# A delta-rule attention fused with a gated feed-forward layer: Gram products, first outputs and weight combinations put at other places of the order

## The chip, the cores and the metric

The kernel runs on one core of a Trainium2 chip. A core has a matrix engine (TensorE, PE in the profile; PEld is its loading of weights), a vector engine (VectorE, DVE), a scalar engine (ScalarE, ACT), a general one (GpSimd, POOL) and a sync engine (SyncE, SP), which here only issues transfers. Each engine runs its own list of instructions in order and waits on semaphores for the others. The metric is the time of one execution on the device in microseconds (us), lower is better.

## The reference

Attention with a state of 48x48 for each of 4 batches and 8 heads, over 768 steps, then a feed-forward layer with 384 inputs and 2048 hidden values:

```python
k_n = k / (np.linalg.norm(k, axis=-1, keepdims=True) + 1e-06)
for t in range(S):
    kt, vt, bt = (k_n[:, :, t], v[:, :, t], beta[:, :, t, None])
    y[:, :, t] = np.einsum('bhd,bhde->bhe', q[:, :, t], state)
    v_old = np.einsum('bhde,bhd->bhe', state, kt)
    state = state + bt[:, :, :, None] * np.einsum('bhd,bhe->bhde', kt, vt - v_old)
x = y.transpose(0, 2, 1, 3).reshape(B * S, H * D)
h = x @ w_in
g = h * (1.0 / (1.0 + np.exp(-1.702 * h)))
return g @ w_out
```

The weights w_in and w_out come as 64-bit floats. The kernel converts them to 32 bits on the device, on their bit patterns.

## The kernel before

**Units.** The 768 steps are cut in 6 chunks of 128. A unit is one chunk of one batch, for all 8 heads; units 0 to 3 are the four batches of the first chunk, units 4 to 7 those of the second, and so on to 23. Two units side by side (256 tokens) make one feed-forward block.

**One unit's work.** `turn` transposes k on PE, and `gram` makes G, the products of all keys of the chunk with each other (16 instructions on PE, then two copies out of PSUM: both on ACT for units 4 to 9, one on ACT and one on DVE for the others). `send_blocks` writes the four 32x32 diagonal blocks of G to DRAM with four transfers, and `load_diagonal` reads them back as `NT`, one block per partition. `invert` inverts them on DVE, for four or two units at a time, in many small steps; the inverses go through DRAM (`Yd`) and come back as `XB`. `Step` then solves for U in four block rows: `solve` multiplies a block row of V by its inverse (psU, copied by ACT to `US`), `below` multiplies by G (psR), and DVE subtracts that from the rows of V below. `queries` and `outputs` make the unit's output (psY) from the masked scores M (`select`, on POOL), and `state` adds to the state ST on DVE. The outputs go to `xT`, for two units together, partly by six small transfers (`xT<-last`).

**Order.** The file writes the order of the engines out by hand. Most operations go through wrappers that keep them in program order (so nearly every row of the profile names line 108); those that are called on `nc.gpsimd` or `nc.sync` directly may be moved by the scheduler, among them the adds of line 764. `together` interleaves the solving of one unit with the products of another; `hops(a, b)` is such a chain of eight for two units. The first four units have no feed-forward work beside them yet: units 0 and 1 are solved first, then 2 and 3. `warm(n)` puts n products whose result nobody reads on PE.

**Background work.** `fill(us)` takes the next pieces of a generator, `background`, until their estimated costs reach the number given: first the conversion of w_in (9 pieces), then the inversion for units 4 to 7 (`invert(1)`), then the conversion of w_out. One conversion (`conversion`) is a step on DVE, a scaling on ACT and four more steps on DVE; `conversions` weaves each piece with the next. Finished pieces set off the fetch of later ones (`fetches`): piece 1 the last quarter of w_in (12 transfers), piece 3 of w_in four row blocks of w_out (`fetch_out`), all on SP.

**Feed-forward.** `hidden` multiplies by w_in and applies the activation; its results go to tiles `gT` from a pool of six (`g_tile`), for the second block partly to `late_g`, which lies in the large scratch tile TW. The first two blocks are multiplied by w_out directly (`both_written`, `written`). From the third on, `seven` does it with seven products of quarter matrices in place of eight, which needs the combinations T1 = W12 - W11, T2 = W22 - T1, T3 = W22 - W12 (in place of W12) and T4 = W21 - T2 (`combined`: 16 adds on POOL). T1, T2 and T4 lie in TW, in its first, second and last third; `KX`, a spare place for a block of k, and the scores of some units lie in TW as well.

**Steady part.** `woven(n)` runs for n from 3 on: outputs of unit n-1, solving of n, scores of n+1, k of unit n+5 (`prepare`; from unit 12 on, k is scaled on POOL by `normalize`) and feed-forward work from `queue`, handed out by `spend`. `follow` issues the next loads and puts the next feed-forward block in the queue; the third block's `hidden` carries the combinations beside it (`beside_of`), one add for each of its steps.

Of the kernel before, what the change touches and what calls it, by code (L numbers as in the profile page):

```python
# [8 lines left out]
F32 = mybir.dt.float32  # L9
# [9 lines left out]
def kernel(  # L19
# [21 lines left out]
    B, H, S, D = q.shape  # L41
# [9 lines left out]
    NB = C // BS  # L51
    HB = 2
    NTH = HB * C
    FQ = 4
    GB = 6
    HF, HM = FC // 2, DM // 2

    XR = DP - D
    NW, NR, NA, NY, NU = 80, 11, 3, 28, 12
# [77 lines left out]
    def warm(n, after=None):  # L137
        ps = ps_moe.tile([128, 256], F32, tag="moe", name="ps_warm")
        if after is not None:
            after(ps[:, 0:1], 0.0)  # L140
        for _ in range(n):
            pe.matmul(ps, lhsT=ones[:, 0:128], rhs=ones, start=True, stop=True)
# [24 lines left out]
    def g_tile():  # L167

        return wk.tile([128, FQ, NTH], F32, tag="gT", name="gT", bufs=GB)
# [39 lines left out]
    def conversion(dst, raw, shape):  # L209

        lo, hi = raw[:, :, :, 0], raw[:, :, :, 1]
        ts, stt = vec.tensor_scalar, vec.scalar_tensor_tensor
        AND, OR = ALU.bitwise_and, ALU.bitwise_or
        E1 = 1 << 20
        p = dst.bitcast(I32)
        ts(p, hi, 0x7FF * E1, None, op0=AND)  # L220
        act.activation(p, p, ACT.Relu, scale=8.0, bias=low)
        yield 0.75
        stt(out=p, in0=hi, scalar=-(1 << 31), in1=p, op0=AND, op1=OR)
        yield 0.95
        ts(hi, hi, E1 - 1, E1, op0=AND, op1=OR)
        yield 0.7
        f = lo.bitcast(F32)
        stt(out=f, in0=lo.bitcast(U32), scalar=2.0**-32, in1=hi, op0=ALU.mult, op1=ALU.add)
        yield 0.95
        stt(out=dst, in0=f, scalar=2.0**-20, in1=dst, op0=ALU.mult, op1=ALU.mult)  # L230
        yield 0.95
# [27 lines left out]
    def conversions():  # L259

        whole = list(pieces())

        def begin(i):
            dst, raw, shape, name = whole[i]
            ops = conversion(dst, places[name[1]] if raw is None else raw, shape)
            return ops, next(ops)

        after, cost = begin(0)
        yield cost
        for i in range(len(whole)):  # L270
            ops = after
            yield next(ops)
            yield next(ops)
            if i + 1 < len(whole):
                after, cost = begin(i + 1)
                yield cost
            yield next(ops)
            cost = next(ops)
            done.add(whole[i][3])
            fetches.pop(whole[i][3], lambda: None)()  # L280
            yield cost
# [22 lines left out]
    def fill(us):  # L304
        while us > 0:
            us -= next(behind, us)
# [107 lines left out]
    def gram(n):  # L414

        c, b = units[n]
        kT = kTs[n]
        G = wk.tile([128, H, 128], F32, tag="G", name="G", bufs=6)
        pool_, tag = (ps_seq, "seq") if c == 0 else (ps_big, "big")
        ps = [pool_.tile([128, NP, 128], F32, tag=tag, name="psG") for _ in range(2)]  # L420
        for h in range(H):
            r = slice(h % 2 * 64, h % 2 * 64 + D)
            pe.matmul(
                ps[h % 2][:, h // 2], lhsT=kT[r, h // 2, :], rhs=kT[r, h // 2, :],
                start=True, stop=True,
            )
        act.activation(G[:, 0::2], ps[0], ACT.Copy)
        if B <= n < 2 * B + HB:
            act.activation(G[:, 1::2], ps[1], ACT.Copy)
        else:  # L430
            vec.tensor_copy(G[:, 1::2], ps[1])
        ready[n] = KN[n % len(KN)], kT, G
        return G

# [28 lines left out]
    def send_blocks(n, others=(), dma=sync):  # L463

        G = ready[n][2]
        Nd = dram.tile([H * C * BS], F32, tag="Nd", name="Nd", bufs=4)
        to = Nd.rearrange("(h p k) -> p h k", p=C, k=BS)
        for blk in range(NB):
            u = slice(blk * BS, (blk + 1) * BS)
            (beside if blk in others else dma)(out=to[u], in_=G[u, :, u])  # L470
        return Nd
# [291 lines left out]
    def add(o, a, b, op, engine=None):  # L763
# [2 lines left out]
    W11, W21 = w_out[:, 0:HF, 0:HM], w_out[:, HF:, 0:HM]  # L766
    W12, W22 = w_out[:, 0:HF, HM:], w_out[:, HF:, HM:]
    T1, T2, T4 = (
        TW[:, i * HF * HM : (i + 1) * HF * HM].rearrange("p (f d) -> p f d", f=HF) for i in range(3)
    )  # L770
    T3 = W12

    def combined():

        n = 2
        for o, a, b in ((T1, W12, W11), (T2, W22, T1), (T3, W22, W12), (T4, W21, T2)):
            for f in range(0, HF, n):
                add(o[:, f : f + n], a[:, f : f + n], b[:, f : f + n], sub_)
                yield

    def beside_of(work, other):

        for cost in work:
            next(other, None)
            yield cost
        run(other)

# [122 lines left out]
    def ahead_of(work, n):  # L910
        for _ in range(n):
            next(work, None)
# [34 lines left out]
    def follow(n):  # L947

        if n + 3 < len(units):
            load(n + 3, ((QP, q),))  # L950
        m = n - 1 + len(KN)
        if n == B + 1:
            nc.sync.dma_start(out=KN[m % len(KN)], in_=KX)
        elif n > B and m < len(units):
            load(m, ((KN, k),), nc.gpsimd.dma_start)
        if n - 1 + B < len(units):
            load_values(n - 1 + B)
        if n % HB == 0 and n > B:
            h = (n - 1) // HB
            gT, sums = [], []  # L960
            work = hidden(xTs[h], gT, slice(0, NTH), 1.3, sums)
            queue.append(beside_of(work, combined()) if h == HB else work)
            queue.append(seven(*units[h * HB], gT, sums))
            xTs.pop(h)

    debt = [0.0]

    def spend(cost):

        debt[0] = debt[0] + cost if queue else 0.0  # L970
        for done in take(debt[0]):
            debt[0] -= done
# [4 lines left out]
    def woven(n, share):  # L977

        nonlocal inverting
        A, B_, D_ = steps.pop(n - 1, None), steps.get(n), steps.get(n + 1) or NoStep()
        m = n + B + 1 if n > B else len(units)
        K = normalize(m) if m < len(units) and m >= 3 * B else iter(())
        P = prepare(m) if m < len(units) else iter(())
        if n == B:
            inverting = invert(*units[2 * B], HB)
        if n % HB == 1 and B + 1 < n and n + 1 + HB < len(units):
            inverting = invert(*units[n + 1 + HB], HB)  # L990
        ahead = FIRST[n] if n in FIRST else STEPS[:3] if n % HB == 1 else STEPS[3:]

        next(K, None)
        together([(B_, 1)], [(A, 2)])
        run(D_.scored)
        next(K, None)
        ahead_of(inverting, ahead[0])
        spend(share / 3)

        together([(A, 3), (D_, 0)], [(B_, 1)])  # L1000
        next(K, None)
        ahead_of(inverting, ahead[1])
        spend(share / 6)
        next(P, None)
        spend(share / 6)

        together([(B_, 2)], [(D_, 0)])
        if A:
            A.queries()
            A.outputs(True)  # L1010
        run(P)
        ahead_of(inverting, ahead[2])
        if n % HB == 0 and n > B:
            run(inverting)
        spend(share / 6)
        next(new_step(n + 2).scored, None)
        spend(share / 6)
        follow(n)
# [69 lines left out]
    pool.memset(late_U[:, H * D :], 0.0)  # L1088
    for s in pair:
        s.select()  # L1090

    def hops(a, b):

        yield [(a, 0)], []
        for blk in range(NB - 1):
            yield [(b, blk)], [(a, blk)]
            yield [(a, blk + 1)], [(b, blk)]
        yield [(b, NB - 1)], []

    def put_out(s):  # L1100
        s.queries()
        s.outputs(True, lambda: fill(1.7))
        steps.pop(s.n)

    path = hops(*pair[:2])
    for i in range(2 * NB):
        together(*next(path))
        if i in (1, 3):
            turn(B + HB + i // 2)
        if i < 2 * NB - 1:  # L1110
            warm(NU // 2 if i in (0, 1, 3) else NU)
        if i > 0:
            fill(1.7)
    for n in (B + 2, B + 3):
        gram(n)
        Ndx.append(send_blocks(n))
    load_diagonals(Ndx)
    for s in pair[:2]:
        put_out(s)
    sync(out=KN[0], in_=KX)  # L1120
    load(8, ((KN, k),), sync)
    for f in range(3):
        fetch_out(f)
    for n in range(B, B + 2):
        load(n, ((QP, q),), sync)
# [7 lines left out]

    gTs = [], []
    ffn.append(hidden(xTs[0], gTs[0], slice(0, NTH), 1.3))
    path = hops(*pair[2:])
    for i in range(2 * NB):
        together(*next(path))
        if i > 2:
            feed()  # L1140
        else:
            warm(NU // 2)
        fill(1.7)
    for s in pair[2:]:
        put_out(s)
# [79 lines left out]
```

## Time and profile before

| what | us |
|---|---|
| median of 3 runs | 781.2 (778.08 to 781.31) |
| the profiled execution | 772.88 |
| its span, first to last instruction | 771.2 |
| PE busy | 728.2 |
| DVE busy | 486.2 |
| ACT busy | 238.7 |
| POOL busy | 237.8 |

The engines in 40 slices of 19.3 us each (a digit is the busy share in tenths, 9 is 90% or more; PEclk is the clock that TensorE was granted):

```profile
PE   9288899989997999999999999999999999999998
PEld 7266778845676888898888988988998988988987
DVE  4896699999677577687677677777766850110000
ACT  3363444533332422322322323323322323212120
POOL 5022001300066442542542632632710601403123
PEclk9579899999998999999999999999999999999999
```

The program opens with units 0 to 3 and the weights' conversion (to about 186 us); from there on the woven part runs to the end. The median of the runs is 8.3 us above the profiled execution; durations below come from the profiled one.

### The profile page before, as it was taken

How to read it: one execution, taken by the hardware profiler on the slowest of the kernel's cores; microseconds unless marked ns; L12 is line 12 of the kernel's file. 1: busy time of each engine (PE TensorE's matmuls, PEld its weight loads, DVE VectorE, ACT ScalarE, POOL GpSimd, SP SyncE). 2: the span in 40 equal slices, each digit the busy share in tenths (PEclk: the TensorE clock that was granted, in tenths of full speed). 3: DMA queues.
4: the chain of work that ended last, by engine and by line, in shares of the span. 5: the costliest groups of instructions: out<-in, count | busy, mean ns of one | idle time of the engine just before them, and what ended most of it. 6: DMA issues, size and time to landing. Idle time of an engine off the chain costs nothing.

```text
span 771.2 us, 19686 instructions
## 1 busy us (share of the span) xinstructions
PE 728.2 (94%) x8451; PEld 624.0 (81%) x8451; DVE 486.2 (63%) x1014; ACT 238.7 (31%) x527; POOL 237.8 (31%) x210
## 2 busy tenths in 40 slices
PE   9288899989997999999999999999999999999998
PEld 7266778845676888898888988988998988988987
DVE  4896699999677577687677677777766850110000
ACT  3363444533332422322322323323322323212120
POOL 5022001300066442542542632632710601403123
PEclk9579899999998999999999999999999999999999
DMA  9985555541222113113113113123122120000000
GB/s 169 150 150 122 157 132 77 133 124 42 51 49 60 35 26 84 37 28 83 36 30 80 36 35 77 36 43 68 37 44 57 22 54 2 2 27 1 26 1 20
DMA packets 128182, 47.11 MB, mean 61 GB/s; under 512 B 117920, under 2 KB 122144, under 8 KB 128096
## 3 DMA queue, kind: packets, MB, share of 16 engines
q1 hardware_dynamic: 125568, 41.54, 26.1%
q0 software_dynamic: 1344, 3.93, 2.3%
q8 instruction: 66, 1.08, 0.6%
q10 hardware_dynamic: 1184, 0.39, 0.2%
q14 instruction: 20, 0.16, 0.1%
HBM read 33.13 MB, written 11.01 MB: 57 GB/s over the span
## 4 chain that ended last, share of the span: by engine, by line
PE 74%; DVE 13%; DMA 4%; issue 3%; SPq 2%; POOL 2%; ACT 1%; ACTq 0%; DVEq 0%; POOLq 0%
PE ph L108 27%; PE po L108 25%; PE psY L108 5%; PE psU L108 4%; PE psQ L108 4%; PE psG L108 3%; DVE w_out L108 3%; PE psT L108 2%; DVE P L108 2%; SPq L108 2%; DVE YB L108 2%; PE ps_warm L108 2%; PE psR L108 2%; DVE w_in L108 1%; DVE V L108 1%
## 5 line engine op out<-in xcount | busy, mean ns | idle before, releaser
L108 PE MATMUL ph<-xT,w_in 128*128 128x256 f32 x1152 | 264.0, 385 | 0.2 <-DMA xT<-last 0.2
L108 PEld LDWEIGHTS ph<-xT,w_in 128*128 128x128 f32 x1152 | 216.0, 191 | 32.4 <-DVE V L108 1.4
L108 PE MATMUL po<-w_out,gT 128*128 128x192 f32 (+1 forms) x736 | 147.2, 354 | 4.1 <-DVE o L108 3.6
L764 POOL TENSOR_TENSOR gT<-gT 128x512 f32<-128x512 f32 x80 | 106.5, 1340 | 124.1 <-ACT gT L108 113.6
L108 DVE TENSOR_TENSOR V<-V,psR 64x384 f32<-64x384 f32 (+1 forms) x96 | 53.3, 556 | 133.9 <-PE psR L108 132.6
L108 PEld LDWEIGHTS po<-w_out,gT 128*128 128x128 f32 x736 | 121.2, 191 | 19.6 <-DVE o L108 4.6
L108 ACT ACTIVATE gT<-ph 128x512 f32<-128x512 f32 x92 | 54.9, 596 | 143.4 <-PE ph L108 143.2
L108 DVE TENSOR_TENSOR P<-NT,YB 64x2 f32<-64x2 f32 (+9 forms) x200 | 95.3, 476 | 6.2
L108 DVE TENSOR_REDUCE YB<-P 64x2 f32<-64x2 f32 (+9 forms) x200 | 81.8, 409 | 6.9
L108 PE MATMUL po<-TW,gT 128*128 128x192 f32 x480 | 83.0, 328 | 0.0
L108 ACT COPY US<-psU 32x384 f32<-32x384 f32 x92 | 43.3, 470 | 127.1 <-PE psR L108 115.9
L108 PEld LDWEIGHTS psU<-V,XB 32*32 32x32 f32 x1536 | 57.0, 105 | 30.6 <-issue 12.7
L108 PEld LDWEIGHTS po<-TW,gT 128*128 128x128 f32 x480 | 77.9, 190 | 1.1 <-issue 0.3
L108 PE MATMUL psU<-V,XB 32*32 32x48 f32 x1536 | 67.8, 202 | 5.7 <-DVE V L108 3.5
L108 PE MATMUL psR<-US,G 32*32 32x48 f32 x2208 | 60.0, 203 | 3.2 <-ACT US L108 3.2
L108 DVE TENSOR_TENSOR o<-o,po 128x192 f32<-128x192 f32 x40 | 13.5, 351 | 75.8 <-PE po L108 75.3
L108 PEld LDWEIGHTS psR<-US,G 32*32 32x32 f32 x2208 | 50.7, 105 | 4.3 <-ACT US L108 3.9
L633 POOL TENSOR_SCALAR_AFFINE_SELECT M<-M 128x1024 f32<-128x1024 f32 x19 | 22.3, 1175 | 92.9 <-DVE M L108 61.0
L108 DVE TENSOR_TENSOR P<-NT 64x512 f32<-64x512 f32 (+7 forms) x50 | 44.5, 890 | 2.0
L93 POOL DMA_DIRECT2D KN<-in_k_dram x12 | 11.5, 958 | 84.1 <-PE psY L108 84.1
L108 PE MATMUL psQ<-QS,kT 48*128 48x176 f32 (+1 forms) x368 | 33.7, 324 | 1.6 <-ACT QS L108 1.6
L108 PE MATMUL psG<-kT 48*128 48x128 f32 x384 | 32.3, 304 | 2.5 <-ACT G L108 2.1
(118 smaller groups left out, 747.1 us busy)
## 6 DMA issues: line engine op xcount, KB each, us to landing
V<-in_v_dram SPq DMA_DIRECT2D x24, 192.0 KB, 3.1
out_dram<-o SPq DMA_DIRECT2D x24, 192.0 KB, 2.4
QP<-in_q_dram SPq DMA_DIRECT2D x22, 192.0 KB, 3.4
raw<-in_moe_w_out_dram SPq DMA_DIRECT2D x9, 384.0 KB, 3.9
NT<-Nd SPq DMA_DIRECT2D x24, 128.0 KB, 2.8
XB<-Yd SPq DMA_DIRECT2D x24, 128.0 KB, 3.1
Nd<-G SPq DMA_DIRECT2D x92, 32.0 KB, 1.7
Yd<-NT SPq DMA_DIRECT2D x22, 128.0 KB, 2.2
```

Of the source, the lines that this page charges most:

```text
L93: dma(out=place(dst, n)[:, :, 0:D], in_=src[b, :, c * C : (c + 1) * C, :].rearrange("h p d -> p h d"),)
L108: return lambda *a, **kw: tc.keep_in_program_order(op(*a, **kw))
L633: (pool if self.n < B else nc.gpsimd).affine_select(out=self.M, in_=self.M, compare_op=ALU.is_gt, fill=0.0, base=0, pattern=[[0, H], [1, 1 ...
L764: (engine or nc.gpsimd).tensor_tensor(o, a, b, op=op)
```

## The change

Seven edits. The scaling on ACT inside a conversion is issued at the beginning of the next fill rather than at the end of the step before it. G of units 0 and 1 lies in two tiles of the gT pool, so that units 6 and 7 find free buffers for theirs. The fetch of w_out's first row block and a fill of 3.3 us stand ahead of the hops. The Gram products of units 6 and 7, with their transfers of blocks, stand inside the hops of units 0 and 1 (after the fifth and sixth), where warming products go. The outputs of unit 0 come ahead of unit 1's last solve, and those of unit 1 after the first solve of unit 2. The hops of units 2 and 3 lose that first one and get longer warming. And T1 and T4 exchange their thirds of TW; the first four adds (T1) are issued in `woven(6)`, and the third block's `hidden` begins with four steps without adds.

```diff
 def conversion(dst, raw, shape):
     ts(p, hi, 0x7FF * E1, None, op0=AND)
+    yield 0.75
     act.activation(p, p, ACT.Relu, scale=8.0, bias=low)
-    yield 0.75
+    yield 0.0
...
 def conversions():
     after, cost = begin(0)
+    next(after)
...
             after, cost = begin(i + 1)
             yield cost
+            next(after)
...
 def gram(n):
-    G = wk.tile([128, H, 128], F32, tag="G", name="G", bufs=6)
+    G = (
+        g_tile().rearrange("p f (o t) -> p (f o) t", o=2) if n < HB
+        else wk.tile([128, H, 128], F32, tag="G", name="G", bufs=6)
+    )
...
 T1, T2, T4 = (
-    TW[:, i * HF * HM : (i + 1) * HF * HM].rearrange("p (f d) -> p f d", f=HF) for i in range(3)
+    TW[:, i * HF * HM : (i + 1) * HF * HM].rearrange("p (f d) -> p f d", f=HF) for i in (2, 1, 0)
 )
...
 def beside_of(work, other):
-    for cost in work:
-        next(other, None)
+    for i, cost in enumerate(work):
+        if i >= FQ:
+            next(other, None)
         yield cost
...
-        queue.append(beside_of(work, combined()) if h == HB else work)
+        queue.append(beside_of(work, combining) if h == HB else work)
...
+combining = combined()
...
 def woven(n, share):
     next(P, None)
+    if n == B + HB:
+        ahead_of(combining, HF // 2)
     spend(share / 6)
...
 for s in pair:
     s.select()
+fetch_out(0)
+fill(3.3)
...
-path = hops(*pair[:2])
+path, later = hops(*pair[:2]), hops(*pair[2:])
 for i in range(2 * NB):
     together(*next(path))
     if i in (1, 3):
         turn(B + HB + i // 2)
-    if i < 2 * NB - 1:
-        warm(NU // 2 if i in (0, 1, 3) else NU)
-    if i > 0:
+    if i in (4, 5):
+        gram(B + HB + i - 4)
+        Ndx.append(send_blocks(B + HB + i - 4))
+    elif i < 2 * NB - 2:
+        warm(NU if i == 2 else NU // 2)
+    if 0 < i < 2 * NB - 1:
         fill(1.7)
-for n in (B + 2, B + 3):
-    gram(n)
-    Ndx.append(send_blocks(n))
+    if i == 2 * NB - 2:
+        put_out(pair[0])
 load_diagonals(Ndx)
-for s in pair[:2]:
-    put_out(s)
+together(*next(later))
+warm(NU // 2)
+put_out(pair[1])
 sync(out=KN[0], in_=KX)
 load(8, ((KN, k),), sync)
-for f in range(3):
+for f in range(1, 3):
     fetch_out(f)
...
-path = hops(*pair[2:])
-for i in range(2 * NB):
-    together(*next(path))
+for i in range(1, 2 * NB):
+    together(*next(later))
     if i > 2:
         feed()
     else:
-        warm(NU // 2)
+        warm(NU)
     fill(1.7)
```

## The prediction

> **What bounds the kernel now.** I read the profile in this order: busy shares and the 40 slices, then busy time by stage, then the chain of waits, then the timelines of single engines around the places where TensorE (PE) is not busy. By stage (columns: stretch in us, length, then busy us and count for PE, PEld, DVE, ACT, POOL, then granted clock, DMA share, GB/s):
>
> ```profile
> 66.00:85.00 19.00, 14.89 (x353) 12.05 (x341) 18.16 (x28) 8.63 (x15) 0.00 (x0) 0.98 0.49 119
> 85.00:94.00 9.00, 9.00 (x158) 8.40 (x162) 3.52 (x8) 3.93 (x11) 0.00 (x0) 0.67 0.77 206
> 94.00:109.00 15.00, 13.54 (x304) 9.98 (x291) 14.17 (x22) 7.79 (x12) 0.00 (x0) 1.00 0.60 150
> 109.00:157.00 48.00, 46.72 (x300) 39.29 (x298) 45.36 (x101) 20.69 (x43) 8.14 (x5) 1.00 0.49 95
> 157.00:186.00 29.00, 25.05 (x223) 15.27 (x225) 26.89 (x66) 8.27 (x17) 1.09 (x1) 0.94 0.33 87
> 242.00:246.00 4.00, 0.03 (x1) 0.00 (x0) 3.63 (x12) 0.60 (x1) 1.31 (x2) 0.82 0.00 0
> 246.00:254.00 8.00, 7.95 (x90) 6.50 (x93) 3.71 (x8) 1.19 (x2) 0.00 (x0) 0.67 0.01 2
> 300.00:771.00 471.00, 464.30 (x5347) 416.07 (x5345) 252.13 (x532) 126.81 (x283) 158.99 (x122) 1.00 0.16 36
> ```
>
> From 300 us on PE is busy 464 of 471 us at clock 1.00: nothing there is touched, and time won earlier is kept. From 66 to 109 DVE paces (the solving hops with weight conversions between them), except 85 to 94, where DVE does 3.5 us of work in 9. From 109 to 157 both PE and DVE are full. At 242 PE stands for 4 us and then runs 8 us at a mean clock of 0.67. These two holes, with DVE's idle time before 66, are what the change can win. DVE's holes, and the work that ends the first stage:
>
> ```profile
> 66.38 1.14 DVE L108 TENSOR_TENSOR V<-V,psR 32x384 f32<-32x384 f32 x2 [7.06 <-PE psR L108]
> ...
> 90.17 0.36 DVE L108 TENSOR_TENSOR ST<-psY,ST 128x192 f32<-128x192 f32 x1 [4.84 <-PE psY L108]
> ...
> 109.14 1.22 DVE L108 TENSOR_TENSOR NT<-NT,bI 128x1024 f32<-128x1024 f32 x1
> ```
>
> **Hops of units 0 to 3 (first part).** The fill of 3.3 us after the masks puts four conversion steps (about 0.6, 0.6, 0.95, 0.9 us start to start, from the same steps at 67.5 to 71.8) into the 7.06 us before 66.38. Their cover is that idle time; their data was fetched before 53 us. The hops keep their pace, one DVE subtraction (1.14 or 0.56 us) and two or three conversion steps, so that I step along DVE's new order with those durations: subtractions at 66.4, 69.7, 72.7, 75.3, 77.7 and 79.7 us (80.45 before). The Gram products of units 6 and 7 (16 products, 1.16 us on PE, two copies of 0.6 on ACT) now stand behind hops 4 and 5. On ACT they stand ahead of the next hop's copy of U, which hop 6 waits for; by the durations that moves hop 6 to 78.8 on PE, while DVE is busy until 79.7: hidden, and 1 us on the path if that cover were gone. 24 warming products (of 84) go; they were fillers. The outputs of unit 0 then run under two fills (2.8 us of steps), its state addition comes at 83.1 instead of 90.17, and unit 1's waits for ACT's copies (0.54 + 0.47 + 0.47) and 1.7 us of PE, which puts it at 86 instead of 91.97. There, DVE idles about 1.6 us in place of 5.9.
>
> What is late next is the transfer of `xT`, for which the first hidden products stand in PE's order ahead of the remaining hops. On SP it stands behind the four loads of w_out and the diagonals:
>
> ```profile
> 82.03 2.35 SPq L108 DMA_DIRECT2D w_out<-in_moe_w_out_dram  x4
> 85.30 5.38 SPq L108 DMA_DIRECT2D Nd<-G  x8
> 90.77 1.79 SPq L108 DMA_DIRECT2D NT<-Nd  x4
> 92.76 4.79 SPq L108 DMA_DIRECT2D xT<-last  x6
> ```
>
> Now it is: eight blocks of units 4, 5, one raw row block, twelve w_in loads (6.7 us, to 75.5), four blocks of unit 6 (its Gram copies end at 77.6, so to 79.5), four w_out loads (to 81.9 in place of 84.4), four blocks, four diagonals, `xT`. The chain of waits shows the last w_out load landing at 90.36, 6.0 us after its issue, so 87.9 now. The fourth diagonal waits for that; `xT` follows at 88.4 and lands 7.06 us later as before (92.76 to the products at 99.82), at 95.4. So hidden products start 4.4 us sooner, and DVE's last subtractions, which then wait for hop 4 behind them, put the first step of the second inversion at 104.2 instead of 109.14. Since PE and DVE are both full after it, I count the lesser: **minus 4.4 us**. Bounds: minus 7 (DVE's order alone, without `xT`, gives 102.1), and 0, if w_out's loads land no sooner than before.
>
> G of units 0, 1 in two buffers of gT costs nothing: the next users of these buffers, hidden products from 95 on, come 10 us after the last reader. Scaling on ACT issued one fill later stands behind the copies of U; its readers on DVE come a hop later (2.0 us at the least, 0.94 for the scaling): 0.
>
> **Combinations of w_out (second part).** Each add takes about 1.0 us on POOL. In the built order two of the first combination's four (those clear of KX) move ahead of unit 5's mask, to where their w_out rows are converted, about 162 us less the gain. There DVE paces and POOL disturbs it: beside one POOL mask of 1.09 us at 179.41 a product of 64x8 took 0.77 us where its neighbours took 0.15 to 0.18. I take 0.6 us for each: **plus 1.2 us**; bounds 0 and 2. The Trainium skill (SBUF — State Buffer, § Who interferes with whom) has the pair of ports shared by these engines locked for a whole instruction; that would be 1 us for each, and the sum 0.8 us later. The trace agrees with the blocking, and shows less than a whole instruction lost.
>
> The mask itself waits for nothing new, and is needed 40 us later (the output products at 221.85). The other two adds and the third combination run between 212 and 222, when POOL did nothing or the same adds, and PE paces. The gain is here:
>
> ```profile
> 227.35 0.97 POOL L93 DMA_DIRECT2D KN<-in_k_dram  x1
> ...
> 231.12 0.83 POOL L320 TENSOR_TENSOR ksq<-KN 128x384 f32<-128x384 f32 x1 [1.76 <-DMA Nd<-G]
> ...
> 240.64 1.67 POOL L325 TENSOR_TENSOR rn<-ssq,half 128x8 f32<-128x8 f32 x1
> 244.99 1.01 POOL L329 TENSOR_TENSOR KN<-KN,rn 128x384 f32<-128x384 f32 x1 [2.68 <-DVE rn L108]
> ```
> ```profile
> 238.92 0.73 DVE L108 TENSOR_TENSOR P<-NT,YB 64x18 f32<-64x18 f32 x1
> ...
> 241.45 0.23 DVE L108 TENSOR_TENSOR P<-NT,YB 64x72 f32<-64x72 f32 x1
> ```
>
> PE waits at 242.03 for unit 12's k, scaled by POOL at 244.99; POOL waits there for DVE's `rn`, which stands behind nine inversion steps. In the new order the load of k is issued after two adds that can run from 223 (unit 5's mask is read by then), at 225 instead of 227.35; it lands 3.8 us later, and four adds follow instead of seven: 228.8 + 0.8 + 4.0 + 1.1 + 1.7 = 236.4 for POOL's power, in place of 242.3. Then POOL is still when DVE's steps run (from 235.3, set by a diagonal that stands where it stood). Four products that took 0.84, 0.74, 0.73 and 0.82 us take 0.16 to 0.19, and the scaling ahead of them 1.22 for 1.55: 2.7 us sooner. PE's wait shrinks from 4.02 to 1.3 us: **minus 2.7 us** (bounds 0 and minus 4). After the wait the clock was 0.50 from 245 to 251, and 18 hidden products took 6.2 us where 3.9 is usual (260.39): with the transposes 2.6 us lost. Waits of 0.67 us (at 289) left the clock at 1.00, one of 3.3 us (165 to 168) did not. At 1.3 us I take the former: **minus 2.6 us**; bounds 0 and minus 2.6.
>
> **Sum.** -4.4 + 1.2 - 2.7 - 2.6 = -8.5 us. The profiled execution took 772.88 us (span 771.2 and 1.7 around it), so 764.4; the median of the runs shown is 781.2, 8.3 above it, and I put the same sum on it: 772.7 us.
>
> **Rivals.** (a) The hole at 242 stays, since the diagonal that DVE waits for until 235.3 doesn't move, and DVE might still be disturbed: only -3.2, 778. Against it: POOL's chain is 6 us shorter. (b) The hops' gain is lost because the transfers ahead of `xT` share the bandwidth (206 GB/s from 85 to 94) and land as late as before: 781.2 + 1.2 - 5.3 = 777. For it: twelve w_in loads now lie just ahead. (c) All bounds at their best: -12.4, 769. (d) The change does not take the adds off the late place: excluded by the built order. (e) Slower: SP's one queue. Diagonals and `xT` wait for w_out's last load. If the twelve w_in loads (1.5 MB) and these four (1.6 MB) shared their way so that they moved at the 119 GB/s of 66 to 85, they would take 26 us from 69, to 95, and `xT` would land at 102.6, 2.8 us late: with the other terms no net effect. At the 87 GB/s of 157 to 186 they end at 104.6 and `xT` lands at 112.1, 12.3 us late: 12.3 + 1.2 - 5.3 = plus 8.2, 789. It decides against the change once the last load lands after 96.4. Against it: the same loads ran at 176 to 352 GB/s when queued together.
>
> **Chances.** Forecast 0.58; (b) 0.12; (a) 0.10; (c) 0.07; (e) 0.08; 0.05 for no net effect. About 0.5% (3.9 us) is what a measurement of this kernel can tell from no change. Faster: forecast, (c) and (b), nearly all: 0.76. Within: (a) and no net effect, 0.16. Slower: 0.08. The range 765 to 780 takes in (a), (b), (c) and leaves out (e) and the tail.
>
> **What would show it.** In the changed profile: conversions on DVE between 59 and 63 us; unit 0's state addition near 83; first hidden products near 95; the second inversion's first step near 104; POOL's power for unit 12 some 6 us ahead of DVE's `rn`; PE's wait before that transpose below 2 us and the clock 1.00 after it. I am wrong if `xT` lands after 99 us, if DVE's conversions between 157 and 186 lengthen by more than 2 us, or if PE still stands 3 us or more at that transpose.

## The result, and the profile after

The changed kernel took 769.8 us (median of 4 executions, 768.4 to 771.2), the kernel before beside it 781.2 us (4 executions, 778.1 to 782.6): a ratio of 0.987, 95% interval 0.983 to 0.991, 11.5 us by the medians. The forecast was 772.7 us, 8.5 us less. Two later repetitions, with many more executions of the kernel before beside them, gave 0.990 each (0.986 to 0.995, and 0.987 to 0.993): some 7.6 us.

The profiled execution of the kernel before (772.9 us) lay 8 us under the median of its own runs, and that of the changed kernel (771.2 us) was the longest of its four, so the two executions set side by side show 1.6 us and not the difference of the medians. That is why the readings below go by differences inside a trace, and by several traces.

Busy time by stage, changed kernel (length, then busy us and count of PE, PEld, DVE, ACT and POOL, granted clock, DMA share, GB/s):

```profile
66.00:85.00 19.00, 16.24 (x366) 13.56 (x367) 14.73 (x23) 8.91 (x16) 1.04 (x1) 0.75 0.79 148
85.00:94.00 9.00, 9.00 (x163) 8.01 (x160) 4.06 (x8) 2.99 (x9) 0.00 (x0) 0.58 0.75 234
94.00:109.00 15.00, 13.39 (x269) 10.10 (x268) 12.86 (x20) 6.11 (x12) 0.00 (x0) 0.89 0.54 126
109.00:157.00 48.00, 48.00 (x316) 40.58 (x316) 45.09 (x100) 21.78 (x45) 8.90 (x5) 1.00 0.49 93
157.00:186.00 29.00, 25.32 (x201) 15.89 (x201) 27.91 (x62) 8.47 (x18) 4.16 (x3) 0.88 0.33 90
242.00:246.00 4.00, 3.20 (x49) 2.47 (x37) 3.53 (x13) 1.55 (x4) 0.00 (x0) 1.00 0.25 49
246.00:254.00 8.00, 6.89 (x122) 5.91 (x124) 5.81 (x12) 1.66 (x3) 1.00 (x1) 1.00 0.01 2
```

The second hole is as forecast: from 246 to 254 the clock is 1.00, not 0.67, and PE stands 1.9 us, not 4.0. In the hops the forecast is not met: the clock is 0.75 from 66 to 85 (0.98 before) and 0.89 from 94 to 109 (1.00 before). DVE's timeline there:

```profile
60.74 0.68 DVE L108 TENSOR_SCALAR w_out<-w_out 128x768 int32<-128x768 int32 x1
61.34 1.49 DVE L108 TENSOR_SCALAR w_in<-w_out 128x768 int32<-128x768 int32 x1
62.76 1.57 DVE L108 SCALAR_TENSOR_TENSOR w_out<-w_out 128x768 f32<-128x768 uint32 x1
64.36 1.72 DVE L108 SCALAR_TENSOR_TENSOR w_in<-w_out,w_in 128x768 f32<-128x768 f32 x1
68.76 1.14 DVE L108 TENSOR_TENSOR V<-V,psR 32x384 f32<-32x384 f32 x2 [2.67 <-PE psR L108]
...
87.15 0.36 DVE L108 TENSOR_TENSOR ST<-psY,ST 128x192 f32<-128x192 f32 x1
93.25 0.36 DVE L108 TENSOR_TENSOR ST<-psY,ST 128x192 f32<-128x192 f32 x1 [4.42 <-PE psY L108]
...
111.73 1.22 DVE L108 TENSOR_TENSOR NT<-NT,bI 128x1024 f32<-128x1024 f32 x1
```

Four conversion steps now fill the idle time ahead of the first subtraction (2.67 us of idling left of 7.06). That subtraction comes 2.4 us later than in the trace of the kernel before (68.76 against 66.38); PE's first products wait for the transfer of the inverses (XB) there, in both kernels. Unit 0's state addition no longer waits, but unit 1's waits 4.42 us for PE's output products, which run at half clock, and the second inversion's first step comes at 111.73 us, where 104.2 was forecast and 109.14 was before (42.97 us behind the first subtraction, 42.76 before). `xT` is late with it. SP's queue:

```profile
83.86 1.78 SPq L108 DMA_DIRECT2D w_out<-in_moe_w_out_dram  x4
85.73 2.70 SPq L108 DMA_DIRECT2D Nd<-G  x4
88.53 4.73 SPq L108 DMA_DIRECT2D NT<-Nd  x4
94.04 4.58 SPq L108 DMA_DIRECT2D xT<-last  x6
```

POOL's list around unit 12, and PE behind it, first in the changed kernel and then in the kernel before:

```profile
228.53 0.97 POOL L93 DMA_DIRECT2D KN<-in_k_dram  x1
...
239.25 2.65 POOL L328 TENSOR_TENSOR rn<-ssq,half 128x8 f32<-128x8 f32 x1
246.05 1.00 POOL L332 TENSOR_TENSOR KN<-KN,rn 128x384 f32<-128x384 f32 x1 [4.15 <-DVE rn L108]
```
```profile
247.11 0.66 PE L108 MATMUL psT<-ident,KN 128*128 128x128 f32 x4 [1.91 <-POOL KN L332]
247.60 4.05 PE L108 MATMUL ph<-xT,w_in 128*128 128x256 f32 x18
```
```profile
246.05 1.12 PE L108 MATMUL psT<-ident,KN 128*128 128x128 f32 x4 [4.02 <-POOL KN L329]
246.96 6.22 PE L108 MATMUL ph<-xT,w_in 128*128 128x256 f32 x18
```

POOL is done with its power at 241.9 and idles 4.15 us until DVE's `rn`: it is DVE that is awaited now. The 18 hidden products take 4.05 us, 6.22 before.

### The profile page after: what moved, and what is told of

It is laid out like the page before. It is cut to its first block, busy times and chain, and to the rows that moved or that the text cites. A ratio compares the mean times of both kernels' runs of the same rounds, so it can differ in the third digit from the quotient of the medians.

```text
span 769.5 us, 19639 instructions
## 1 busy us (share of the span) xinstructions
PE 729.1 (95%) x8427; PEld 625.3 (81%) x8427; DVE 489.3 (64%) x1014; ACT 238.7 (31%) x527; POOL 242.3 (31%) x210
## 4 chain that ended last, share of the span: by engine, by line
PE 73%; DVE 16%; issue 3%; POOL 3%; DMA 3%; SPq 1%; ACT 0%; DVEq 0%; POOLq 0%; ACTq 0%
PE ph L108 27%; PE po L108 24%; PE psY L108 6%; PE psU L108 5%; DVE P L108 4%; DVE w_out L108 3%; PE psQ L108 3%; DVE YB L108 3%; PE psG L108 2%; PE ps_warm L108 2%; PE psR L108 2%; DVE NT L108 2%; PE psT L108 2%; DVE raw L108 1%; SPq L108 1%
## 5 line engine op out<-in xcount | busy, mean ns | idle before, releaser
L108 PEld LDWEIGHTS psU<-V,XB 32*32 32x32 f32 x1536 | 59.8, 108 | 30.0 <-issue 15.9
L108 PE MATMUL psU<-V,XB 32*32 32x48 f32 x1536 | 70.4, 207 | 5.5 <-DVE V L108 3.0
L108 PE MATMUL psR<-US,G 32*32 32x48 f32 x2016 | 55.8, 205 | 3.6 <-ACT US L108 3.6
L108 PEld LDWEIGHTS psR<-US,G 32*32 32x32 f32 x2016 | 47.2, 106 | 4.6 <-ACT US L108 4.3
L93 POOL DMA_DIRECT2D KN<-in_k_dram x12 | 11.5, 958 | 81.6 <-PE psY L108 81.6
L108 DVE TENSOR_REDUCE NT<-P 64x32 f32<-64x512 f32 (+9 forms) x50 | 33.4, 668 | 1.7
```

Source lines behind the costliest of these rows:

```text
L93: dma(out=place(dst, n)[:, :, 0:D], in_=src[b, :, c * C : (c + 1) * C, :].rearrange("h p d -> p h d"),)
L108: return lambda *a, **kw: tc.keep_in_program_order(op(*a, **kw))
```

## The experiments

Each run gave a trace. To read them together I cut each into four pieces: **a** from the first subtraction of the hops to the second inversion's first step, **b** from there to unit 5's output products (those of its masked scores, `psY<-TW,US`), **c** from there to unit 12's transposes, **d** from there to the end of the span (us); ahead of them the mean granted clock from 64 to 112 us. The time ahead of the first subtraction is in no piece: it was 66.2 to 70.5 us, and PE's first products wait there for XB to land, in the kernel before too (1.39 and 0.82 us in its second trace, where it was 68.1).

```
kernel                       clock    a      b      c      d     ratio to before (95%)
before, first trace          0.93  42.76 112.71  24.20 525.15
before, second (b_again)     0.83  46.47 112.86  24.13 525.14   0.999 (0.995 to 1.003)
before + warming (b_warm)    1.00  42.33 112.62  23.64 525.31   0.999 (0.996 to 1.002)
before + warming at unit 12  0.89  43.12 113.74  24.11 522.52   0.994 (0.991 to 0.997)
combinations only            0.93  42.70 113.07  21.77 522.47   0.993 (0.988 to 0.997)
hops' part only              0.96  40.69 112.60  24.03 524.88   0.994 (0.991 to 0.998)
changed, first trace         0.79  42.97 113.64  21.74 522.39   0.987 (0.983 to 0.991)
changed, second (a_again)    0.93  38.77 113.69  21.74 522.50   0.990 (0.986 to 0.995)
changed, third (a_third)     0.86  39.66 114.77  21.79 522.48   0.990 (0.987 to 0.993)
changed, xT first (a_xt)     0.82  41.22 114.83  21.99 522.45   0.991 (0.988 to 0.994)
changed, no fill (a_nofill)  0.79  46.10 114.25  21.75 522.54   0.995 (0.992 to 0.998)
changed + 24 (a_keep)        0.96  38.51 113.68  21.76 522.73   0.987 (0.983 to 0.992)
changed + warming (a_warm)   1.00  37.90 113.69  21.74 524.07   0.987 (0.982 to 0.991)
changed + both (a_best)      1.00  37.82 113.66  21.75 522.48   0.985 (0.981 to 0.990)
```

**Both kernels once more.** No edit.

> The kernel before, unchanged, for a second trace and the spread of its times. Its profiled execution was 772.9 us, some 8 below its median of 781.2, so its trace may be of an untypical execution. Theory A (the two edits of the forecast, about -4 each, on a typical execution): this trace is again near 773 or near 780, and if near 780 the further 7 to 8 us lie outside the stretches 56 to 112 and 240 to 254, as a lower granted clock spread over the span. Theory B (the hops' part is what typical executions gain from): near 780, with the further time between 56 and 112 us (second inversion's first step at 114 or later, not 109.1). Ratio 1.000 within 0.4%.

> The changed kernel, unchanged, for a second trace. Theory A and theory B alike: a profiled execution near 770 us; the second inversion's first step between 109 and 113 us (111.7 in the first trace), PE's wait ahead of unit 12's transpose under 2.5 us and the granted clock 1.00 after it. Ratio to the kernel before 0.985 to 0.992.

Measured: the kernel before 774.4 us (773.8 to 779.8) here, 776.2 over the 11 executions beside it (772.7 to 783.0); the changed kernel 768.5 (766.2 to 773.9). The profiled execution of the kernel before took 778.4 us this time, and of the 5.5 us that it had more than in the first trace 3.7 are in **a** and 1.7 ahead of it. So the further time lay where theory B had put it, between 56 and 112 us, with the second inversion at 114.57. For the changed kernel the ratio, the wait of 1.70 us ahead of unit 12's transpose and the clock behind it are as expected; the second inversion came sooner, at 106.57. Busy time in slices of 4 us, second trace of the kernel before, and DVE's last subtractions there:

```profile
96.00:100.00 4.00, 3.06 (x98) 2.10 (x98) 3.84 (x8) 1.79 (x3) 0.00 (x0) 1.00 0.19 50
100.00:104.00 4.00, 3.40 (x82) 2.37 (x76) 3.94 (x6) 0.98 (x2) 0.00 (x0) 0.82 0.63 151
104.00:108.00 4.00, 4.00 (x45) 2.88 (x41) 2.70 (x4) 2.73 (x4) 0.00 (x0) 0.50 1.02 317
108.00:112.00 4.00, 4.00 (x38) 2.88 (x34) 2.38 (x4) 1.13 (x3) 0.00 (x0) 0.50 0.39 48
```
```profile
108.90 0.56 DVE L108 TENSOR_TENSOR V<-V,psR 32x384 f32<-32x384 f32 x1 [1.85 <-PE psR L108]
113.10 0.56 DVE L108 TENSOR_TENSOR V<-V,psR 32x384 f32<-32x384 f32 x1 [1.79 <-PE psR L108]
114.57 1.22 DVE L108 TENSOR_TENSOR NT<-NT,bI 128x1024 f32<-128x1024 f32 x1
```

The clock falls a second time at about 103 us, PE becomes the slower one of the pair, and DVE waits 1.85 and 1.79 us for products it did not wait for in the first trace. The instructions are the same: whether the clock falls in the hops differs from execution to execution. This second fall goes with 3.7 us. What a fall costs seems to depend on its place: in the kernel before with warming at unit 12 the clock fell a second time too, from 96 to 103 us, and **a** was 43.12, hardly longer. In the changed kernel the same piece took 42.97 us at a mean clock of 0.79 and 38.77 at 0.93.

**One part alone.** Combinations only, against the kernel before (the hops' part alone is the changed kernel with these lines put back):

```diff
-        ... for i in range(3)
+        ... for i in (2, 1, 0)
-        for cost in work:
-            next(other, None)
+        for i, cost in enumerate(work):
+            if i >= FQ:
+                next(other, None)
-            queue.append(beside_of(work, combined()) if h == HB else work)
+            queue.append(beside_of(work, combining) if h == HB else work)
+    combining = combined()
         next(P, None)
+        if n == B + HB:
+            ahead_of(combining, HF // 2)
```

> Only w_out's combinations as in the change; Gram products, outputs, fetches and conversions of the hops as before. Theory A (forecast's terms): -2.7 (wait ahead of unit 12's transpose) -2.6 (half clock behind it) +1.2 (two additions beside the conversions of 157 to 186) = -4.1 us, 777; PE's wait under 2.5 us at that transpose. Theory B (the gain comes from the hops): -1 to +1 us. Theory C (the traces as they stand: 111.7 against 109.1 at the second inversion, and 5 us won at units 6 and 12): all of the gain is here, -8 to -11 us, 770 to 773.

> Only the hops' part: units 6 and 7's Gram products, the outputs of units 0 and 1, the fetches and the conversions moved as in the change; w_out's combinations where they were. Theory A: -4.4 us, 777; second inversion's first step 3 to 5 us sooner than in the repeated trace of the kernel before. Theory B: -7 to -11 us, 770 to 774. Theory C: -1 to +3 us, 780 to 784, and PE still stands 3.5 us or more ahead of unit 12's transpose, with a granted clock near 0.7 behind it.

Measured: 769.8 us and 772.3 us, where the kernel before took 776.2: about 5.7 and 4.6 us by the ratios (expected: 4.1 and 4.4). Together that is 10.3, where the changed kernel in the same round gained 7.6; each interval is some 6 to 7 us wide, so the times do not give the size of a part. Each part gains by itself, and theory C, which the first two traces had suggested, falls: the hops' part alone is faster. With the combinations alone **c** and **d** are those of the changed kernel and **a** is that of the kernel before; with the hops' part alone it is the other way round.

**The half clock behind the wait, by itself.**

```diff
         spend(share / 6)
+        if n == 2 * B - 1:
+            warm(30)
         next(P, None)
```

> The kernel before, with 30 warming products (some 3.7 us on PE) just ahead of unit 12's transpose, where PE stands for 4 us: the wait itself stays, the clock behind it should not fall. It parts the two terms of the combinations' gain. If the half clock is a cost of its own (theory A): the transposes and 18 hidden products behind the wait take 4.7 us instead of 7.3, granted clock 1.00 over 8 us behind the wait, and the kernel is 2.6 us faster (1.5 to 3). Rival: the half clock comes all the same, or the wait's release moves by the warming: 0, or up to 1 us slower.

Measured: 771.5 us against 774.9, ratio 0.994 (0.991 to 0.997). PE's timeline of this kernel:

```profile
243.80 3.44 PE L108 MATMUL ps_warm<-ident 128*128 128x256 bf16 x30
248.08 0.66 PE L108 MATMUL psT<-ident,KN 128*128 128x128 f32 x4 [0.84 <-POOL KN L329]
248.57 4.05 PE L108 MATMUL ph<-xT,w_in 128*128 128x256 f32 x18
```

**c** stays at 24.11, so the wait is as long as before, only filled; **d** falls from 525.1 to 522.5. The forecast's term for the half clock, 2.6 us, is shown as a cost of its own.

**More warming in the hops.** The kernel before, then the changed kernel:

```diff
-            warm(NU // 2 if i in (0, 1, 3) else NU)
+            warm(9 if i in (0, 1, 3) else NU)
         Ndx.append(send_blocks(n))
+        warm(NU)
-            warm(NU // 2)
+            warm(NU if i < 2 else 2 * NU)
```
```diff
             Ndx.append(send_blocks(B + HB + i - 4))
+            warm(4)
-            warm(NU if i == 2 else NU // 2)
+            warm(NU if i == 2 else 9)
     together(*next(later))
-    warm(NU // 2)
+    warm(NU)
-            warm(NU)
+            warm(NU if i == 1 else 2 * NU)
```

> The kernel before, with more warming products in both sets of hops (9 for 6 behind hops 0, 1 and 3 of the first set, 12 behind each of the two Gram products, 12 and 24 for 6 in the second set's first three hops). Repeated runs of the kernel before spread over 773 to 783 us; its second trace (776.7) differs from its first (771.2) by half clock from 103 to 113 us. If falls of the granted clock for want of PE work make that spread (theory A), then no half clock between 96 and 113, at most 2 us of it between 80 and 96, all executions within 772 +- 2 us and a median 3 to 4 us below the kernel before. Rival (the falls have nothing to do with how much PE does there): the same spread, 774 to 783, median within 1 us or slower by the products' own time, 3 us.

> The changed kernel, with more warming products in both sets of hops (9 for 6 behind hops 0, 1, 3; 4 behind the two Gram products; 12 for 6 ahead of unit 1's outputs; 24 for 12 in the wait for the extra rows of xT). Theory A: the changed kernel also loses 2 to 5 us to half clock in the hops (trace 1: 80 to 92 and 104; trace 2: 79 to 86), so its executions come within 765 +- 2 us, second inversion's first step at 106 or sooner, 2 to 3 us faster than the changed kernel. Rival: no change of the clock, median 768 to 770; or PE's longer hops cost 2 us.

Measured: the clock is 1.00 from 64 to 112 us in both traces. The changed kernel took 765.5 us (763.7 to 767.1), ratio 0.987, with **a** at 37.90: as theory A had it. The kernel before took 772.8 us, ratio 0.999 with 1 in its interval: no gain shown. Its **a** is 42.33, hardly under the first trace's 42.76, so the fall at 84 to 91 us there cost next to nothing. That the second fall makes its spread is not settled by this run: 10 of its 12 executions came within 771.5 and 774.2 us (of the kernel before beside it, 10 of 29 came up to 774.2), but two took 775.7 and 780.1, and those were not traced.

**The 24 products that the change took out.** Put back behind the Gram products of units 6 and 7:

```diff
             Ndx.append(send_blocks(B + HB + i - 4))
+            warm(NU)
```

> The changed kernel once more, unchanged, as the measure for the three runs beside it. 768 to 770 us, ratio to the kernel before 0.987 to 0.992; half clock somewhere between 78 and 93 us, as in its two traces so far.

> The changed kernel, with the 24 warming products that it took out put back (12 behind each of the Gram products of units 6 and 7). The forecast called them fillers that cost nothing to lose. If that step is wrong (theory A): the granted clock stays 1.00 from 76 to 92 us, unit 1's state addition comes 3.1 us behind unit 0's (3.7 and 6.1 in the two traces of the changed kernel), second inversion's first step 38 to 39 us behind the first subtraction, time 1 to 3 us below the changed kernel beside it. Rival: 24 products are not what decides (the fall comes all the same, 0 us), or they delay unit 0's outputs by their own 3 us: 0 to 2 us slower.

Measured: 768.8 us without them, 766.4 with them (5 of 6 executions at 764.6 to 766.5, where 2 of 10 without them came under 766.6); the ratios are 0.990 and 0.987, and their intervals overlap, so the size of 2.4 us is a reading of the medians. So a gain from these 24 alone is likely, but not shown. In the trace the clock is 1.00 from 72 to 112 (it had been at half from about 67 to 71), unit 1's addition comes 3.1 us behind unit 0's, and **a** is 38.51: each as theory A had it. But one of the three traces without them had 38.77. In the third trace of the changed kernel the clock was at half from 66 to 76 and from 90 to 93, only in part where it was expected.

**What the second inversion waits for.** First the loads of `xT` ahead of the diagonals, then the changed kernel without the fill ahead of the hops:

```diff
-    load_diagonals(Ndx)
     together(*next(later))
     warm(NU // 2)
     put_out(pair[1])
+    load_diagonals(Ndx)
```
```diff
     fetch_out(0)
-    fill(3.3)
```

> The changed kernel, with the six loads of xT's extra rows ahead of the four diagonals on SP's queue, not behind them. The forecast says that the first hidden products wait for that transfer and that this wait sets the second inversion. Then the loads are issued at some 89.5 instead of 91.2 us and land by 93 to 94 instead of 97: hidden products 2 to 3 us sooner, second inversion's first step 1 to 2 us sooner (relative to the first subtraction of the hops), time 1 to 2 us less. Rival: DVE's conversions pace the hops by then, nothing changes behind 100 us: 0. Or the diagonals come late for the second inversion: 1 to 2 us slower.

> The changed kernel without the fill of 3.3 us ahead of the hops: four steps of weight conversion come later again, DVE idles 7 us ahead of the first subtraction as before. The forecast holds that the transfer of xT and not DVE's order sets the hidden products. If so, 0 to 1 us slower, or up to 0.5 faster, since those steps ran beside POOL's masks at up to twice their time and with them the masks. Rival (DVE's order is what the second inversion waits for): the 3.3 us come back in full, 3 us slower.

Measured: 769.2 us with `xT` first, so no gain shown (768.5 and 768.8 for the changed kernel in its repetitions, all in rounds of their own); the 1 to 2 us expected would be within the intervals. In its trace the six loads were issued only at 91.35 us, when unit 1's outputs had just been copied (from 90.95 on), and these were late, with the clock at half from 80 to 91; the diagonals were not what held the loads there. In the second trace of the changed kernel the outputs were copied from 89.41 on and the loads, behind the diagonals, issued at 91.20. So this run leaves open what an earlier `xT` is worth where the clock stays up. Without the fill the kernel took 772.5 us, 3.7 more than the changed kernel beside it, and the rival of that expectation holds: 3 us slower. DVE's timeline without the fill:

```profile
107.08 0.56 DVE L108 TENSOR_TENSOR V<-V,psR 32x384 f32<-32x384 f32 x1
107.67 1.83 DVE L108 SCALAR_TENSOR_TENSOR w_in<-w_out,w_in 128x768 f32<-128x768 f32 x2
109.53 0.69 DVE L108 TENSOR_SCALAR w_out<-w_out 128x768 int32<-128x768 int32 x1
110.14 0.34 DVE L108 TENSOR_SCALAR w_out<-raw 128x384 int32<-128x384 int32 x1
110.40 0.95 DVE L108 SCALAR_TENSOR_TENSOR w_out<-w_out 128x768 f32<-128x768 uint32 x1
111.39 0.96 DVE L108 SCALAR_TENSOR_TENSOR w_in<-w_out,w_in 128x768 f32<-128x768 f32 x1
112.26 1.22 DVE L108 TENSOR_TENSOR NT<-NT,bI 128x1024 f32<-128x1024 f32 x1
```

The inversion is taken up only when all of w_in is converted, and 4.6 us of conversion now stand between the last subtraction and its first step, where 1.9 stood in the changed kernel (109.86 to 111.73). DVE's own work paces the end of this stretch. The first trace of the changed kernel has the same mean clock, 0.79, as this one, so the 3.1 us between their pieces **a** (42.97 and 46.10) are hardly the clock's.

**Both at once.** The changed kernel with the further warming of the hops, and 12 products ahead of unit 12's transposes:

```diff
         spend(share / 6)
+        if n == 2 * B - 1:
+            warm(NU)
         next(P, None)
```

> The changed kernel with the further warming products of the hops (9 for 6, 4 behind the Gram products, 12 for 6, 24 for 12) and 12 more ahead of unit 12's transpose, where the wait of 1.9 us left the clock at 1.00 in two traces and let it fall in a third (the end came 524.1 us behind the transpose there, 522.5 in the others). Theory A: 764 us, 4 to 5 below the changed kernel beside it, 522.5 us behind the transpose. Rival: the further products cost as much as they save, 0 to 1 us.

Measured: 765.3 us (763.8 to 766.8), ratio 0.985 (0.981 to 0.990), 3.5 us by the medians below the changed kernel beside it: the lowest median of all these kernels, though not told apart from those with further warming alone (765.5, in another round) or with the 24 products (766.4). DVE's timeline of it:

```profile
66.39 1.14 DVE L108 TENSOR_TENSOR V<-V,psR 32x384 f32<-32x384 f32 x2 [1.73 <-PE psR L108]
...
83.77 0.36 DVE L108 TENSOR_TENSOR ST<-psY,ST 128x192 f32<-128x192 f32 x1
86.88 0.36 DVE L108 TENSOR_TENSOR ST<-psY,ST 128x192 f32<-128x192 f32 x1 [1.43 <-PE psY L108]
...
104.21 1.22 DVE L108 TENSOR_TENSOR NT<-NT,bI 128x1024 f32<-128x1024 f32 x1
```

With the first subtraction at the same place as in the first trace of the kernel before (66.39 and 66.38), the second inversion starts at 104.21. That is what the forecast said of the changed kernel; it is reached in this one, where the clock does not fall.

## Why the forecast was right, and where it was not

By the pieces of the traces, and for the hops by traces whose clock stayed at 1.00:

- **Hops, -4.4 us.** 42.33 to 37.82: -4.5. The places are met too (unit 0's addition 83.1 forecast, 83.77 measured; unit 1's 86 and 86.88; first hidden products 95.4 and 93.96; inversion 104.2 and 104.21), but in the kernel with more warming, not in the changed one. There **a** was 42.97, 38.77 and 39.66, so it gave back 1 to 5 us. The kernel before lost time to falls as well (42.76 and 46.47): the means of the plain traces, 44.6 and 40.5, differ by 4.1. That the changed kernel's own gain came near the forecast's 4.4 thus rests partly on luck, since the forecast had no term for falls in either.
- **Two additions beside conversions, +1.2 us.** **b** is 113.07 with the combinations alone against 112.6 to 112.9: +0.3. With both parts it is 113.6 to 114.8 against 112.60: +1.0 to +2.2. The kernel before with warming at unit 12 had 113.74 without any such addition, so the term is not clear of what varies anyway. DVE's work from 157 to 186 grew by 1.0 us (26.89 to 27.91; 27.41 with the hops' part alone), within the forecast's limit of 2.
- **Shorter wait, -2.7 us.** **c** falls from 24.0 to 21.75: -2.3. PE still stood 1.9 us, not 1.3. The four products that POOL had drawn out to 0.73 to 0.84 us take 0.16 to 0.19, as forecast. The scaling ahead of them does not: it took 1.89 us, where 1.22 was forecast and 1.55 was before, with POOL's mask and power still running beside it (238.20 to 241.90, the scaling from 238.48). POOL's power is done 4.15 us ahead of DVE's `rn`, not 6.
- **Half clock behind it, -2.6 us.** **d** falls from 525.1 to 522.5: -2.6, and filling the wait with other work gives the same.

With the hops at clock 1.00 and +1.0 for the additions the sum of these is about -8.4, the forecast -8.5, the three measured ratios make it -7.7 to -10.2 of 781. That the first comparison showed 11.5 us is a matter of its four executions of the kernel before (778 to 783): over the later ones the median was 775 to 776.5. Two slips of the working change nothing: all bounds at their best make -13.6, not the -12.4 of rival (c), which keeps the 1.2; and the wait before 168 us is 3.17 us in its row, not 3.3.

**The step that failed** is "24 warming products (of 84) go; they were fillers". It counted them by their time on PE, which is indeed spare, and gave them no price. Put back, they brought about 2.4 us by the medians, which is not clear of the noise. With more products still, and 12 ahead of unit 12, it was 3.5 us in the same round: none of the 6 executions was above 766.9, and 8 of the 10 without were above 768.0. The working clock was read from the hops of the kernel before, with those products in them, and was carried over to hops without them. The forecast's own sign of error ("if `xT` lands after 99 us") did show in the first trace (100.81), by way of that clock, and not in the second (96.97).

**The limit named was also too simple.** "What is late next is the transfer of `xT`" was right as to when it is issued: 88.4 us forecast, 88.81 in the kernel with both kinds of warming. But there DVE was at work almost all the way from 87.75 us to the second inversion (15.51 of 16.46 us), with waits for PE of only 0.17 and 0.22 us. And taking the fill away cost 3.7 us. The conversions of w_in on DVE hold the second inversion at least as firmly; the forecast had this only as the far end of its range (102.1). Without its 2.3 us of waits, 1.4 of them for unit 1's outputs, that trace comes to 101.9. So the agreement at 104.2 is closer than the working behind it.

**The rivals.** (b), hops without a gain, is what the first pair of traces shows; with the hops' part alone at 0.994 (0.991 to 0.998) it is refuted. (a) is refuted by **c** and **d**. (c), all bounds at their best, would fit the first 11.5 us; the 7.6 us of the later rounds and the pieces speak against it. (e), a late last load of w_out, did not occur: the four loads were issued by 85.6 in the first trace, and `xT` (94.04) followed unit 1's outputs (copied from 93.64 on). What stays open is what makes the longest executions of the kernel before (780 to 784): one fall of the clock went with some 4 us, another with next to nothing, and no execution above 778.4 was traced.

## What to carry to other kernels

Filler products on TensorE may not be free to remove: look at what clock the stretch has with them, and price their removal by a run with them put back. Here more of them kept the clock at 1.00 in the traces and took 3.5 us off the changed kernel; for the kernel before no gain showed. Where one trace of a kernel lies well off the median of its runs, take a second before reading differences of a few us out of two, and compare pieces inside a trace. Where two resources end a stretch within 2 us of each other, name both; taking one away alone may then show nothing.

## What the runs showed of the hardware

**The clock fell without a long wait.** Second trace of the changed kernel, around the fall:

```profile
72.00:76.00 4.00, 2.96 (x108) 2.49 (x107) 3.85 (x5) 1.34 (x4) 0.00 (x0) 1.00 0.89 237
76.00:78.00 2.00, 1.33 (x30) 1.14 (x32) 1.92 (x4) 1.37 (x3) 0.00 (x0) 1.00 1.04 209
78.00:80.00 2.00, 2.00 (x42) 1.94 (x36) 1.93 (x3) 1.21 (x3) 0.00 (x0) 0.69 1.03 195
80.00:84.00 4.00, 3.35 (x52) 2.97 (x52) 3.76 (x8) 2.28 (x4) 0.00 (x0) 0.50 0.75 146
```

PE was busy 4.29 of the 6 us ahead of the fall, and its longest wait from 67 us on was 1.04 us. On the other hand PE stood 1.91 us ahead of unit 12's transposes in the first trace of the changed kernel with the clock staying at 1.00, and 1.92 us in the changed kernel with more warming in the hops, where it fell and 18 hidden products took 5.74 us instead of 4.05. The length of one wait does not decide it. The Trainium skill (TensorE: Matmul & The Clock Gate, § What's actually happening) ties the clock to activity in windows of about 3.4 us that run free of the program; the traces agree that the fall is not tied to the program, since the same list fell at other places in other executions. It says that an idle window of that length brings the clock down; ahead of this fall no wait came near it, and the nearer description is that of the same page's § A second HAM failure mode: psum-queue depth-cycling, where small gaps between groups of products, in another kernel, make the clock go to and fro (HAM is that page's name for what sets the clock).

**DVE and POOL slowed each other.** Beside POOL's masks the second, third and fourth conversion steps of the fill took 1.49, 1.57 and 1.72 us where they take 0.68, 0.94 and 0.96 at other places (the forecast had taken these), and the masks took longer as well, 4.08 us for three and 1.80 for one (3.20 and 1.10 before):

```profile
61.20 4.08 POOL L108 TENSOR_SCALAR_AFFINE_SELECT M<-M 128x1024 f32<-128x1024 f32 x3
65.23 1.80 POOL L108 TENSOR_SCALAR_AFFINE_SELECT TW<-TW 128x1024 f32<-128x1024 f32 x1
```

DVE still had 2.67 us of idle time behind it, in which the first subtraction waited for PE, and so no cost of it shows: the fill was still worth 3.7 us.
